# Transposing r and k of two chunks on TensorE in a fused RWKV-6 and feed-forward kernel, with a new instruction order

## The chip, the cores and the metric

The kernel runs on one core of a Trainium2 chip. Its time is the device time in microseconds of one execution. The kernel before took 179.31 us, the median of three runs (179.21 to 180.19).

## What is computed

For each batch and head, a linear attention with a decaying state runs over 768 positions; its output, all heads of a position side by side, goes through two matrix products with a leaky ReLU between them. The sizes are 4 batches, 8 heads, 768 positions and a head width of 48, so a row is 384 wide; the inner width is 2048.

```python
for t in range(S):
    cur = einsum('bhd,bhe->bhde', u * k[t], v[t])
    y[t] = einsum('bhd,bhde->bhe', r[t], state + cur)
    state = w[t][..., None] * state + einsum('bhd,bhe->bhde', k[t], v[t])
x = y.transpose(0, 2, 1, 3).reshape(3072, 384)
h = x @ w_in                      # 384 -> 2048
out = maximum(0.01 * h, h) @ w_out
```

All tensors are float32 in memory; the kernel computes its products in bfloat16.

## The kernel before

**Chunks.** The 3072 rows are cut into 24 chunks of 128 positions, numbered from zero in the order in which they are worked on (four batches take turns). Chunks 0 to 3 are worked on in pairs (`pair`), chunks 4 to 23 by `single`. The steps of a chunk are named here by the chunk and a short word: 6.k is the step of chunk 6 that makes its scaled k.

What a single chunk does, with the profile's lines and the engine:

- Four loads, w, k, r and v (L708, issued by SyncE), into one buffer `in`; lw, the logarithm of w (L718, ScalarE).
- cum: the running sums as a product (L724) and the chunk's totals (L727), TensorE; a: their exponentials (L745, ScalarE); ci: the sums less one position (L736, VectorE); two exponentials into PSUM (L750, L754, ScalarE).
- r and k: r and k times these exponentials (`mult`, L407, VectorE), into one tile `rk` of 128 positions by 2 x 512 in bfloat16 (each head is padded from 48 to 64).
- Then r and k are transposed into `rkT`, in one of two ways. On TensorE (`transposes`): four transposes of 128x128 for r and four for k (L418), each kind into one PSUM bank, and a copy out of PSUM for each kind, by VectorE (L423) or ScalarE (L425). Or by one DMA (L771) issued by SyncE, which transposes the whole of `rk` into `rkT`. The set `RK_DMA` names the chunks that go by DMA.
- scores: products of rkT's halves (L864), for one chunk or for two merged ones (10 with 11, 12 with 13 and others); two masks m (L795, VectorE); sb: the state scaled by a (L782, GpSimd); sums: k times v (L805, TensorE); state: sums plus sb (L820, VectorE; for a batch's first chunk a copy, L818); intra: the chunk's output (L831, L836, TensorE).
- The part of u: two products on GpSimd (L437, L441), their sum dg (L445, VectorE), vs: that times v (L449, GpSimd); vb: v in bfloat16 (L457, GpSimd).
- y: intra plus vs (L482, VectorE), its transposes (L468, TensorE) and the copy into xT (L473 VectorE or L475 ScalarE); six late chunks do this by DMA (L849).

**Blocks.** The feed-forward part goes by 14 blocks B0 to B13 of one or two chunks. A block has up products (L1030, into PSUM; the leaky ReLU by ScalarE, L1045) and down products (L1060, groups of four matmuls, then a copy into `o`, L1071 or L1073). Blocks B7 to B13 use, in place of the eight plain quarter products, seven products of sums and differences of quarters (L960, TensorE), with the sums made by VectorE (L941; in the weights once, L910, four steps) and the results taken by ScalarE and VectorE (L976, L974, L981). Weights come by DMA and are cast to bfloat16 (L340 to L344) by GpSimd, VectorE or ScalarE.

**Order.** All of it is cut into some 1,100 steps in `Plan`, each with the engine it may run on. The list `ORDER`, written out by number, gives the order in which the steps are emitted, so on each engine's queue the order of its steps; the table `FORCE` names the engine of a step that could run on several. A buffer is given to a step when it is emitted: eight PSUM banks `ps`, eleven buffers `in`, five `rk`, four `rkT`, and others. An engine takes its steps strictly in order and waits at one whose inputs or buffer are not ready. `Plan.order` also keeps times of its own for each step; they choose among free buffers and set the number of idle products that keep TensorE busy in the first 24 us.

Of the kernel before, what the change touches and what calls it, by code (L numbers as in the profile page):

```python
# [22 lines left out]
class Plan:  # L23
# [76 lines left out]
ORDER = [1122, 0, 1, 2, 3, 4, 5, 6, 7, 11, 14, 20, 12, 18, 15, 17, 16, 13, 19, 21, 8, 22, 25, 26, 27, 23, 36,  # L100
# [67 lines left out]
def kernel(  # L168
# [25 lines left out]
    RK_DMA = {6, 11, 12, 14, 15, 16, 17, 18, 19, 20, 21, 22, 23}  # L194
# [939 lines left out]
```

## Time and profile before

| | |
|---|---|
| median of three runs (lowest, highest) | 179.31 us (179.21, 180.19) |
| the profiled execution, first to last instruction | 177.0 us |
| mean granted TensorE clock | 1.000 |
| TensorE, its weight loads, VectorE, ScalarE, GpSimd busy | 96%, 79%, 81%, 64%, 61% |
| DMA transposes of rk | 13, a median of 3.8 us from issue to landing |
| moved by DMA | 34.25 MB, 115885 packets |

The profile names an execution's span from its first to its last instruction; the time of a run is longer by what lies around that. A group's row gives line, engine, operation, the tiles written and read, and their form; then the count, the busy time, the mean duration of one in nanoseconds, and the engine's idle time just before, with what ended it. A row of a timeline gives start, duration, and in brackets the idle time before. A matmul's end is modelled, since matmuls are pipelined: the drawn duration of one is longer than what it costs in a dense run. "PEld" is the loading of weights into TensorE, "SPq" the issuing of DMAs by SyncE.

### The profile page before, as it was taken

The numbers are of one execution on the slowest core, as the hardware profiler recorded it, in microseconds if no ns is written. First come the engines' busy times: TensorE is split into PE (matmuls) and PEld (weight loads), VectorE is DVE, ScalarE is ACT, GpSimd is POOL, SyncE is SP. The second block draws the span as 40 slices with busy tenths as digits, with TensorE's granted clock in tenths as the row PEclk, the third lists the DMA queues.
The fourth block names the chain that finished last, engine by engine and source line by source line (L and its number), as shares of the span: only waits on it lengthen the run. The fifth ranks groups of instructions, "written<-read, shape, count | busy, mean of one in ns | idle before, by whom it ended". The sixth has DMA issues, their size and how long they took to land.

```text
span 177.0 us, 5530 instructions
## 1 busy us (share of the span) xinstructions
PE 170.4 (96%) x2155; PEld 139.9 (79%) x2158; DVE 143.5 (81%) x299; ACT 114.0 (64%) x263; POOL 107.3 (61%) x143
## 2 busy tenths in 40 slices
PE   7999999999999999999999999999999998999993
PEld 2566779867768877777779899899899997799992
DVE  7498935267599899889879999999999999956662
ACT  5676769734677794796379964676769950178500
POOL 5989946486749859879599093391693959100000
PEclk9999999999999999999999999999999999999999
DMA  5999999999999999999999999996999897432104
GB/s 138 261 271 340 350 300 195 351 231 199 201 206 195 191 199 227 163 201 179 198 206 195 197 208 209 163 222 124 210 194 196 188 226 78 118 101 80 44 26 157
DMA packets 115885, 34.25 MB, mean 194 GB/s; under 512 B 108305, under 2 KB 115090, under 8 KB 115858
## 3 DMA queue, kind: packets, MB, share of 16 engines
q1 hardware_dynamic: 115856, 33.89, 93.1%
q8 instruction: 17, 0.28, 0.7%
q14 instruction: 10, 0.08, 0.2%
q10 hardware_dynamic: 2, 0.00, 0.0%
HBM read 25.17 MB, written 4.72 MB: 169 GB/s over the span
## 4 chain that ended last, share of the span: by engine, by line
PE 69%; DVE 15%; ACT 5%; issue 4%; DMA 3%; POOL 2%; DVEq 0%; SPq 0%; ACTq 0%
PE ps L1030 30%; PE ps L1060 13%; PE ps L960 10%; DVE rk L407 3%; DMA rkT<-rk 3%; PE ps L864 3%; DVE in L941 2%; PE ps L418 2%; ACT g L425 2%; PE ps L724 1%; PE ps L836 1%; DVE ci L736 1%; PE ps L518 1%; DVE dg L445 1%; ACT ps L750 1%
## 5 line engine op out<-in xcount | busy, mean ns | idle before, releaser
L1030 PE MATMUL ps<-xT,w_in_b 128*128 128x256 bf16 (+1 forms) x672 | 70.8, 258 | 0.3 <-DVE rk L407 0.2
L1045 ACT ACTIVATE g<-ps 128x512 bf16<-128x512 f32 x96 | 54.4, 598 | 18.1 <-PE ps L1030 16.0
L1030 PEld LDWEIGHTS <-w_in_b 128*128 128x128 bf16 x672 | 56.9, 98 | 7.8 <-issue 0.6
L437 POOL TENSOR_TENSOR ru<-in,ub 128x384 f32<-128x384 f32 x24 | 24.3, 1017 | 13.1 <-DMA in<-in_k_dram 7.0
L1060 PE MATMUL ps<-w_out_b,g 128*128 128x384 bf16 x160 | 31.4, 326 | 0.0
L407 DVE TENSOR_TENSOR rk<-in,ps 128x384 bf16<-128x384 f32 x48 | 24.8, 547 | 6.1 <-ACT ps L754 2.3
L782 POOL TENSOR_TENSOR sb<-s,a 128x384 bf16<-128x384 f32 x18 | 15.6, 875 | 16.6 <-ACT a L745 8.1
L795 DVE TENSOR_TENSOR m<-ps,maskb 128x512 bf16<-128x512 f32 x40 | 25.1, 682 | 0.3 <-PE ps L864 0.2
L441 POOL TENSOR_TENSOR ru<-ru,in 128x384 f32<-128x384 f32 x24 | 23.8, 1000 | 2.1 <-DMA in<-in_r_dram 1.1
L1060 PEld LDWEIGHTS <-g 128*128 128x128 bf16 x160 | 14.1, 97 | 6.8
L449 POOL TENSOR_TENSOR vs<-in,dg 128x384 f32<-128x384 f32 x20 | 17.4, 874 | 3.0 <-DMA in<-in_v_dram 2.1
L960 PEld LDWEIGHTS <-g 128*128 128x128 bf16 x224 | 18.3, 98 | 0.2
L976 ACT COPY o<-ps 128x192 f32<-128x192 f32 x18 | 5.8, 320 | 17.5 <-PE ps L960 15.5
L960 PEld LDWEIGHTS <-in 128*128 128x128 bf16 x168 | 13.6, 98 | 1.9 <-DVE in L941 1.4
L445 DVE TENSOR_REDUCE dg<-ru 128x8 f32<-128x384 f32 x24 | 12.9, 545 | 1.9 <-POOL ru L441 1.7
L457 POOL CAST vb<-in 128x384 bf16<-128x384 f32 x24 | 12.7, 534 | 2.2 <-DMA in<-in_v_dram 2.2
L981 DVE TENSOR_TENSOR o<-ps,o 128x192 f32<-128x192 f32 x35 | 11.6, 351 | 1.9 <-ACT o L976 1.1
L482 DVE TENSOR_TENSOR y<-ps,vs 128x384 bf16<-128x384 f32 x20 | 10.9, 553 | 2.4 <-PE ps L836 2.3
L754 ACT ACTIVATE ps<-ci 128x384 f32<-128x384 f32 x20 | 9.8, 493 | 4.7 <-DVE ci L736 4.1
L718 ACT ACTIVATE lw<-in 128x384 bf16<-128x384 f32 x20 | 9.9, 521 | 4.1 <-DMA in<-in_w_dram 4.1
L736 DVE TENSOR_TENSOR ci<-ps,lw 128x384 f32<-128x384 f32 x20 | 10.9, 551 | 1.8 <-PE ps L724 1.1
L960 PE MATMUL ps<-in,in 128*128 128x192 bf16 x112 | 11.4, 247 | 0.5 <-DVE in L941 0.5
(105 smaller groups left out, 258.8 us busy)
## 6 DMA issues: line engine op xcount, KB each, us to landing
out_dram<-o SPq DMA_DIRECT2D x23, 192.0 KB, 2.8
in<-in_w_dram SPq DMA_DIRECT2D x20, 192.0 KB, 4.7
in<-in_k_dram SPq DMA_DIRECT2D x20, 192.0 KB, 4.2
in<-in_r_dram SPq DMA_DIRECT2D x20, 192.0 KB, 4.2
in<-in_v_dram SPq DMA_DIRECT2D x20, 192.0 KB, 4.1
in<-in_moe_w_out_dram SPq DMA_DIRECT2D x4, 768.0 KB, 6.9
in<-in_moe_w_in_dram SPq DMA_DIRECT2D x2, 768.0 KB, 9.7
in<-in_moe_w_in_dram SPq DMA_DIRECT2D x4, 384.0 KB, 8.1
```

Source lines behind the costliest of these rows:

```text
L407: (nc.gpsimd if e == "POOL" else nc.vector).tensor_tensor(out=o, in0=x, in1=i, op=ALU.mult)
L437: lambda e: nc.gpsimd.tensor_tensor(out=ru.t[:], in0=kv(), in1=ubv, op=ALU.mult),
L441: lambda e: nc.gpsimd.tensor_tensor(out=ru.t[:], in0=ru.t[:], in1=rv(), op=ALU.mult),
L445: lambda e: nc.vector.tensor_reduce(out=dg.t[:], in_=ru.t[:], axis=AX.X, op=ALU.add),
L449: lambda e: nc.gpsimd.tensor_tensor(out=vs.t[:], in0=vv(), in1=dg.t[:].unsqueeze(2).to_broadcast([128, H, D]), op=ALU.mult),
L457: {"POOL": 0.56}, lambda e: nc.gpsimd.tensor_copy(out=vb.t[:], in_=vv()),
L782: lambda e: nc.gpsimd.tensor_tensor(out=sb.t[:].rearrange("p g a d -> p (g a) d"), in0=s_in.t[:].rearrange("p g a d -> p (g a) d"), in1=a_ ...
L795: lambda e, par=par: nc.vector.tensor_tensor(out=m.t[:, par, :, :], in0=sc[par].t[:].rearrange("p (g t) -> p g t", g=NP), in1=maskb[:].uns ...
L960: nc.tensor.matmul(o(), lhsT=x()[:, i, :], rhs=y()[:, i, :], start=fresh, stop=(stop and i == ii[-1]), skip_group_check=True)
L1030: nc.tensor.matmul(hp.t[:, a * N : (a + 1) * N], lhsT=w_in_b[:, t, (j + a) * 128 : (j + a + 1) * 128], rhs=xb.t[:, t, 0:N], start=(a == 0 ...
L1045: lambda e, hp=hp, g=g, j=j, J=J, N=N: nc.scalar.activation(out=g.t[:, j : j + J, 0:N], in_=hp.t[:, 0 : J * N].rearrange("p (a n) -> p a n ...
L1060: nc.tensor.matmul(op.t[:, 0:DM], lhsT=g.t[:, j, off : off + 128], rhs=w_out_b[:, j, :], start=(j == 0), stop=(j == NJ - 1))
```

## The change

Chunks 11 and 12 leave the set of those that are transposed by DMA:

```diff
-    RK_DMA = {6, 11, 12, 14, 15, 16, 17, 18, 19, 20, 21, 22, 23}
+    RK_DMA = {6, 14, 15, 16, 17, 18, 19, 20, 21, 22, 23}
```

For each of the two, one DMA step becomes four steps: transposes of r, a copy, transposes of k, a copy. The numbers of all later steps move up by three, then by six, and `ORDER` and `FORCE` are written anew:

```diff
-ORDER = [1122, 0, 1, 2, 3, 4, 5, 6, 7, 11, 14, 20, 12, 18, 15, 17, 16, 13, 19, 21, 8, 22, 25, 26, 27, 23, 36,
...
+ORDER = [1128, 0, 1, 2, 3, 4, 5, 6, 7, 11, 14, 20, 12, 18, 15, 17, 16, 13, 19, 21, 8, 22, 25, 26, 27, 23, 36, 40, 24,
...
-    "POOL", 122: "POOL", 124: "POOL", 126: "POOL", 128: "ACT", 129: "POOL", 131: "ACT", 132: "POOL", 134: "DVE",
-    135: "ACT", 137: "POOL", 138: "POOL", 140: "POOL", 141: "POOL", 143: "POOL", 144:
...
+    120: "POOL", 122: "POOL", 124: "POOL", 126: "POOL", 128: "ACT", 129: "POOL", 131: "ACT", 132: "POOL", 134: "DVE",
+    135: "ACT", 137: "POOL", 138: "POOL", 140: "ACT", 141: "ACT", 143: "POOL", 144: "DVE", 158: "ACT", 160: "DVE",
...
```

(Rows of `ORDER` and `FORCE` are shortened here.) Apart from the numbers, the first 201 entries of `ORDER` are the same; they reach to about 40 us. Behind them every engine's order differs, SyncE's excepted: its queue has the same steps in the same order, without the two DMA transposes. All four new copies out of PSUM are ScalarE's. Other steps also change engine: of the older copies of rkT five go from ScalarE to VectorE and three the other way; of those into xT three and two; of the copies into `o` (L1071, L1073) three from VectorE to ScalarE and one back; two states from VectorE to ScalarE; three copies of results (L976) from ScalarE to VectorE; two weight casts from GpSimd to ScalarE, and one from ScalarE to VectorE.

By name, the stretches of the queues that the prediction speaks of (dn1 is the second quarter of a block's down products, up4 its up products from the fifth on):

```text
TensorE from about 36 us
 before  4.scores B0.dn1 B2.dn1 B1.dn1 B0.dn2 5.tr 4.intra 4.sums B2.dn2 6.cum B1.dn2 B0.dn9 4.tr_y 5.tr B0.dn10
         B3.up4 B3.up12 B3.up0 B0.dn11 B1.dn3 7.cum 5.scores B0.dn3 B3.up8 B3.dn0 5.intra 7.tr B2.dn3 5.sums 7.tr
         B3.dn1 5.tr_y 8.cum 7.scores
 after   4.scores B0.dn1 B2.dn1 B0.dn9 B1.dn1 5.tr 4.intra 4.sums 5.tr B1.dn2 4.tr_y 5.scores B0.dn2 6.cum B0.dn10
         B3.up4 B3.up0 B2.dn2 B0.dn11 7.cum B1.dn3 B2.dn3 B3.up12 B3.dn0 B3.up8 B3.dn1 5.intra 5.sums B3.dn2 8.cum
         7.tr 7.tr 5.tr_y B3.dn3
VectorE from about 38 us
 before  5.r 5.copy 4.y 4.state 5.k 5.dg 6.ci 4.xT 5.copy 6.k 6.r 6.dg B0.o 7.ci 5.m 5.m 7.k 7.r 7.dg 5.y
 after   5.r 5.k 4.y 5.copy 4.xT 5.m 5.m 6.ci cast 5.dg 6.k 7.ci 6.r B1.o B2.o B0.o 7.k 7.r 5.y
GpSimd, chunks 10 to 14
 before  10.sb 11.ru 11.ruk 10.ru 10.ruk 13.ru 13.ruk 11.sb 10.vs 10.vb 12.ru 12.ruk 11.vs 11.vb 17.ru 12.sb 14.ru
         13.sb 14.ruk 12.vb 12.vs 13.vb 13.vs
 after   10.ru 10.ruk 11.sb 13.ru 10.sb 11.ru 10.vb 11.ruk 10.vs 12.sb 11.vb 11.vs 13.ruk 14.ru 12.ru 13.sb 12.ruk
         14.ruk 12.vb 12.vs 13.vb 13.vs
VectorE after, in the same stretch
         6.state 13.ci 11.m 10.m 11.m 13.k 10.m 13.r 12.ci 12.r 11.dg 10.y 12.k 10.xT 11.y L910 11.xT 13.dg 9.state
         11.state 12.m 12.m 13.m 14.ci 12.dg 15.ci 14.k 14.dg 14.r 13.m 13.state 13.y
```

(ru and ruk are L437 and L441.) In the order before, all four L910 steps stand behind 9.dg; in the new one they are spread over the stretch up to chunk 17. At the end, from 23.intra on, TensorE has the same products, with B12's and B13's up products in another order.

More of the change, by code (lines that the diff above doesn't have):

```diff
@@ L99 @@
 TY = (0.95, 24, 0.7, -0.6)
-ORDER = [1122, 0, 1, 2, 3, 4, 5, 6, 7, 11, 14, 20, 12, 18, 15, 17, 16, 13, 19, 21, 8, 22, 25, 26, 27, 23, 36,
[53 rows of a table removed]
-FORCE = {4: "ACT", 6: "DVE", 24: "ACT", 27: "ACT", 30: "DVE", 33: "ACT", 47: "ACT", 57: "ACT", 59: "DVE", 60:
-    "ACT", 62: "DVE", 80: "ACT", 83: "ACT", 86: "DVE", 89: "ACT", 103: "ACT", 113: "DVE", 115: "DVE", 116:
-    "DVE", 118: "DVE", 120: "POOL", 122: "POOL", 124: "POOL", 126: "POOL", 128: "ACT", 129: "POOL", 131: "ACT",
-    132: "POOL", 134: "DVE", 135: "ACT", 137: "POOL", 138: "POOL", 140: "POOL", 141: "POOL", 143: "POOL", 144:
-    "ACT", 158: "ACT", 160: "DVE", 169: "DVE", 173: "DVE", 187: "DVE", 189: "DVE", 198: "DVE", 202: "DVE", 238:
-    "ACT", 240: "ACT", 254: "DVE", 262: "ACT", 278: "ACT", 280: "ACT", 294: "ACT", 310: "DVE", 312: "ACT", 326:
-    "DVE", 342: "DVE", 344: "DVE", 378: "ACT", 386: "ACT", 422: "ACT", 424: "DVE", 438: "ACT", 446: "DVE", 495:
-    "ACT", 503: "ACT", 607: "ACT", 615: "ACT", 739: "ACT", 745: "DVE", 759: "ACT", 773: "DVE", 787: "DVE", 801:
-    "ACT", 823: "ACT", 829: "DVE", 851: "ACT", 857: "DVE", 885: "ACT", 888: "ACT", 893: "ACT", 921: "ACT", 924:
-    "ACT", 929: "ACT", 957: "ACT", 960: "ACT", 965: "ACT", 993: "ACT", 996: "ACT", 1001: "ACT", 1029: "ACT",
-    1032: "ACT", 1037: "DVE", 1065: "ACT", 1068: "ACT", 1073: "DVE", 1107: "DVE", 1110: "ACT", 1115: "ACT"}
@@ new lines @@
+ORDER = [1128, 0, 1, 2, 3, 4, 5, 6, 7, 11, 14, 20, 12, 18, 15, 17, 16, 13, 19, 21, 8, 22, 25, 26, 27, 23, 36, 40, 24,
[49 rows of a table added]
+FORCE = {4: "ACT", 6: "DVE", 24: "ACT", 27: "ACT", 30: "DVE", 33: "ACT", 47: "ACT", 57: "ACT", 59: "DVE", 60: "ACT",
+    62: "DVE", 80: "ACT", 83: "ACT", 86: "DVE", 89: "ACT", 103: "ACT", 113: "DVE", 115: "DVE", 116: "DVE", 118: "DVE",
+    120: "POOL", 122: "POOL", 124: "POOL", 126: "POOL", 128: "ACT", 129: "POOL", 131: "ACT", 132: "POOL", 134: "DVE",
+    135: "ACT", 137: "POOL", 138: "POOL", 140: "ACT", 141: "ACT", 143: "POOL", 144: "DVE", 158: "ACT", 160: "DVE",
+    169: "ACT", 173: "DVE", 187: "DVE", 189: "ACT", 198: "ACT", 202: "DVE", 238: "DVE", 240: "DVE", 254: "ACT", 262:
+    "ACT", 278: "DVE", 280: "DVE", 294: "ACT", 310: "ACT", 312: "DVE", 326: "ACT", 342: "DVE", 344: "DVE", 365: "ACT",
+    367: "ACT", 381: "DVE", 389: "DVE", 405: "ACT", 407: "ACT", 428: "ACT", 430: "ACT", 444: "ACT", 452: "DVE", 501:
+    "ACT", 509: "ACT", 613: "ACT", 621: "DVE", 745: "ACT", 751: "DVE", 765: "DVE", 779: "DVE", 793: "ACT", 807: "ACT",
+    829: "ACT", 835: "ACT", 857: "ACT", 863: "ACT", 891: "ACT", 894: "ACT", 899: "DVE", 927: "ACT", 930: "ACT", 935:
+    "DVE", 963: "ACT", 966: "ACT", 971: "ACT", 999: "ACT", 1002: "DVE", 1007: "ACT", 1035: "ACT", 1038: "ACT", 1043:
+    "DVE", 1071: "ACT", 1074: "ACT", 1079: "DVE", 1113: "DVE", 1116: "ACT", 1121: "ACT"}
```

102 rows, old and new, of the table ORDER are left out of this document.

## The prediction

> **What bounds the kernel now.** I read the page's busy times first, then the chain that ended last, then groups by form, then five places along the time axis.
>
> ```profile
> PE 170.4 (96%) x2155; PEld 139.9 (79%) x2158; DVE 143.5 (81%) x299; ACT 114.0 (64%) x263; POOL 107.3 (61%) x143
> DMA  5999999999999999999999999996999897432104
> PE 69%; DVE 15%; ACT 5%; issue 4%; DMA 3%; POOL 2%; DVEq 0%; SPq 0%; ACTq 0%
> 34.66 0.45 PE ps L418 x8
> 97.38 2.62 PE ps L1030 x24
> 166.09 7.93 PE ps L960 x96
> ```
>
> TensorE holds 69% of the chain. In the chain's dense pieces it issues without a hole: 2.62 us for 24 up products is 109 ns for 256 columns, 7.93 us for 96 products is 83 ns for 192, 0.45 us for 8 transposes is 56 ns for 128. All three are 0.43 ns a column, so the number of columns sets TensorE's time, and a transpose costs 56 ns wherever TensorE never waits. The DMA engines are nearly as full until about 145 us. The next view is by stretches (PE, PEld, DVE, ACT, POOL busy):
>
> ```profile
> 40.00:50.00 10.00, 9.69 (x115) 6.96 (x113) 7.14 (x16) 6.26 (x16) 7.48 (x9) 1.00 1.14 208
> 130.00:140.00 10.00, 10.00 (x129) 9.11 (x127) 9.82 (x21) 9.02 (x26) 6.95 (x8) 1.00 1.03 186
> 140.00:150.00 10.00, 9.82 (x141) 8.88 (x139) 9.97 (x18) 3.87 (x11) 8.12 (x12) 1.00 0.97 165
> ```
>
> From 130 to 150 us VectorE is as full as TensorE (19.8 of 20 us): there VectorE's backlog decides. Where TensorE does wait, the timeline shows it:
>
> ```profile
> 44.31 0.83 PE L1030 MATMUL ps<-xT,w_in_b 128*128 128x128 bf16 x12 [0.16 <-DVE rk L407]
> 46.94 0.82 PE L1060 MATMUL ps<-w_out_b,g 128*128 128x384 bf16 x4
> 47.69 0.83 PE L1030 MATMUL ps<-xT,w_in_b 128*128 128x128 bf16 x12
> 48.35 0.81 PE L1060 MATMUL ps<-w_out_b,g 128*128 128x384 bf16 x4
> 49.20 0.49 PE L836 MATMUL ps<-vb,m 128*128 128x48 bf16 x8
> 49.81 0.40 PE L418 MATMUL ps<-ident,rk 128*128 128x128 bf16 x4
> 150.38 0.84 PE L960 MATMUL ps<-in,in 128*128 128x192 bf16 x8 [0.53 <-DVE in L941]
> 151.61 0.83 PE L960 MATMUL ps<-w_out_b,in 128*128 128x192 bf16 x8 [0.40 <-DVE in L941]
> ```
>
> A matmul's end is modelled about 0.16 us behind the next one's earliest start (8 products of L960 are drawn as 0.84 us, but cost 8 x 83 ns = 0.66), so each hole is about 0.16 us longer than shown: 0.70 and 0.56 us at 150, 1.26 together. At 44 to 50 the holes are 0.32 at 44.31, then, from the starts (four down products cost 0.65 us, 12 half-width ups 0.66), 0.10 at 47.69, 0.20 at 49.20 and 0.4 at 49.81: 1.0 us. That is 2.3 us of waits behind the part that both orders share. Smaller ones are left out.
>
> **The transposes.** The two chunks' 16 transposes cost 16 x 56 ns = +0.9 us on TensorE, and nothing hides that: the number of the other matmuls is the same. Their four copies out of PSUM all go to ScalarE:
>
> ```profile
> L425 ACT COPY rkT<-ps 128x512 bf16<-128x512 bf16 x7 | 4.0, 590 | 0.9 <-PE ps L418 0.9
> L423 DVE COPY rkT<-ps 128x512 bf16<-128x512 bf16 x7 | 2.9, 420 | 4.4 <-PE ps L418 4.4
> L771 SPq DMA_TRANSPOSE rkT<-rk x13: 1232/1282/2201, 46.1 to 147.5; - x13
> 75.42 2.20 SPq L771 DMA_TRANSPOSE rkT<-rk  x1
> 77.72 1.15 SPq L708 DMA_DIRECT2D in<-in_k_dram  x2
> 81.76 2.11 SPq L771 DMA_TRANSPOSE rkT<-rk  x1
> ```
>
> Four times 590 ns is 2.4 us on an engine that is 64% busy; ScalarE's slack hides it, and without that slack it would cost 2.4. They also take four turns of the eight PSUM banks, for which no row here gives a price: from 0 to one hole of the size at 150 (0.70 us); I take 0, as no hole in the list stands at a transpose of r and k except at 49.81. SyncE loses two issues of 2.20 and 2.11 us (chunks 11 and 12) and the waits in front of them; the loads behind them keep their order and can start up to 4.3 us earlier. Nothing on TensorE waits for those loads directly, so I book no gain here, only that loads are not late (see the second rival). The Trainium skill, on the page VectorE: DVE Perf Modes, section The three transpose paths, gives 390 ns for a 128x128 transpose on TensorE and 1309 ns by DMA. By that, 16 would cost 6.2 us in place of 0.9, and the time would come out near 184; the row of eight in 0.45 us decides against it, since here they are issued back to back; I leave it a chance under 0.01.
>
> **The engines that change hands** in the new order: on VectorE two more copies of rkT (L423, 420 ns), one more of xT, one weight cast and three copies of L976 against two states and two o copies fewer: +0.6 us in all. ScalarE takes two weight casts from GpSimd (0.83 us each), ahead of a copy of 5's k and of 6.lw; there it sat idle:
>
> ```profile
> 39.42 0.52 ACT L718 ACTIVATE lw<-in 128x384 bf16<-128x384 f32 x1 [1.92 <-DMA in<-in_w_dram]
> ```
>
> The 1.92 us hold both casts; without that wait 5.scores would come up to 1.7 us later. SyncE's order is the same except for the two removed issues.
>
> **The order at 40 to 52 us.** VectorE's own idle time there:
>
> ```profile
> 43.70 0.56 DVE L407 TENSOR_TENSOR rk<-in,ps 128x384 bf16<-128x384 f32 x1 [1.04 <-ACT ps L754]
> 45.47 0.55 DVE L407 TENSOR_TENSOR rk<-in,ps 128x384 bf16<-128x384 f32 x1 [1.22 <-DMA in<-in_r_dram]
> 46.62 0.55 DVE L445 TENSOR_REDUCE dg<-ru 128x8 f32<-128x384 f32 x1 [0.59 <-POOL ru L441]
> 48.01 1.28 DVE L795 TENSOR_TENSOR m<-ps,maskb 128x512 bf16<-128x512 f32 x2
> 49.21 1.01 DVE L407 TENSOR_TENSOR rk<-in,ps 128x384 bf16<-128x384 f32 x2
> ```
>
> These are 6.k, 6.r and 6.dg, which wait for chunk 6's loads: 2.85 us idle. The new order moves 5.scores in front of 6.cum, so that both masks of chunk 5 (1.28 us, now at 48.01) and a weight cast (about 0.56) stand in front of 6.k and fill the wait, and 7.ci stands in front of 6.r. I take 1.5 of the 2.85 as saved (the bounds are 0 and 2.85; 7.ci waits for 7.cum, so not all). On TensorE, one more down product (0.65) stands in front of 5.intra, and 5.intra, 5.sums, a down product and 8.cum in front of 7's transposes, which covers the 0.20 and the 0.4; I take 0.7 of the 1.0 us as gone.
>
> **The order from 52 to 152 us.** I added up, from the mean durations, the work that each order puts ahead of a step on its own engine. TensorE's work ahead of the product at 150.38, less VectorE's work up to the difference that it reads: 15.7 us before, 15.6 after. For the one at 151.61: 15.3 and 16.2. TensorE's holes up to there equal VectorE's idle time less this lead, up to a constant. Before, the holes came to 1.0 + 0.7 = 1.7 at the first and 2.3 at the second. VectorE's idle time falls by 1.5 early and, I estimate, rises by 0.5 in the new, tight GpSimd stretch below: 1.0 less. So the first product's holes come to 1.7 + 0.1 - 1.0 = 0.8, the second's to 2.3 - 0.9 - 1.0 = 0.4, which the 0.8 covers. What remains is 0.8 or 0.9 of 2.3 us: -1.4. After 23.intra both orders run the same products, at full rate (the 96 above).
>
> **The sum.** +0.9 - 1.4 = -0.5 us. The profiled execution spans 177.0 us; the median of the three runs is 179.31, so 2.3 us lie around the span, which the change does not touch. 176.5 + 2.3 = 178.8 us. Half a per cent, 0.9 us, is about what a measurement of this kernel can tell from no change.
>
> **Rivals.** First, the whole 2.3 us goes, because VectorE's backlog is gone by 150: 177.0 + 0.9 - 2.3 + 2.3 = 177.9. For it speaks the full 2.85 us of early idle time; against it the lead at the first product, which does not grow. The Trainium skill points the same way: Perfetto Trace Analysis, section Identifying the Most-Contended Engine, says to judge TensorE by its weight loads and not by matmul time. By its 79% there would be room for 16 transposes at no cost, and with all holes gone the time would be 177.0; the dense rows at 0.43 ns a column leave no such room, and I give it 0.03, inside this rival's chance.
>
> Second, slower, by GpSimd. The new order moves 6.sums from 58 us to about 71 (12.7 us more TensorE work ahead), so 6.state ends near 74, and 10.sb, which waits for it, stands in GpSimd's queue ahead of 17 more steps of chunks 10 to 14.
>
> ```profile
> L437 POOL TENSOR_TENSOR ru<-in,ub 128x384 f32<-128x384 f32 x24 | 24.3, 1017 | 13.1 <-DMA in<-in_k_dram 7.0 <-issue 6.0
> L441 POOL TENSOR_TENSOR ru<-ru,in 128x384 f32<-128x384 f32 x24 | 23.8, 1000 | 2.1 <-DMA in<-in_r_dram 1.1
> L449 POOL TENSOR_TENSOR vs<-in,dg 128x384 f32<-128x384 f32 x20 | 17.4, 874 | 3.0 <-DMA in<-in_v_dram 2.1 <-DVE dg L445 0.9
> L457 POOL CAST vb<-in 128x384 bf16<-128x384 f32 x24 | 12.7, 534 | 2.2 <-DMA in<-in_v_dram 2.2
> L782 POOL TENSOR_TENSOR sb<-s,a 128x384 bf16<-128x384 f32 x18 | 15.6, 875 | 16.6 <-ACT a L745 8.1 <-ACT g L1045 4.6 <-DVE s L818 2.3
> 88.19 0.50 POOL L457 CAST vb<-in 128x384 bf16<-128x384 f32 x1 [0.91 <-DMA in<-in_v_dram]
> L736 DVE TENSOR_TENSOR ci<-ps,lw 128x384 f32<-128x384 f32 x20 | 10.9, 551 | 1.8 <-PE ps L724 1.1 <-PE ps L727 0.4 <-ACT a L745 0.2
> L482 DVE TENSOR_TENSOR y<-ps,vs 128x384 bf16<-128x384 f32 x20 | 10.9, 553 | 2.4 <-PE ps L836 2.3
> L910 DVE TENSOR_TENSOR in<-w_out_b 128x1536 bf16<-128x1536 bf16 x2 | 2.3, 1174 | 0.0
> ```
>
> Up to 13.vs that is 3 ru, 4 of L441, 3 sb, 4 vb and 4 vs: 3.05 + 4.00 + 2.63 + 2.14 + 3.50 = 15.3 us. VectorE's work from 6.state to 13.y, which needs 13.vs, is 4 ci, 8 masks, 6 rk, 4 dg, 2 y, 2 xT copies, one difference of L910 and 3 states: 17.8 us by the means, less some 0.08 for each of 30 that overlap (two masks in 1.28), 15.4. There is no slack, so 0.5 us of VectorE waits is in my sum. In this queue 12.vb comes 12.6 us behind 6.state, at 86.6; its load came at 88.1 before. If the two SyncE issues that are gone do not bring that load forward, VectorE loses 1.6 us there and TensorE gets it back as holes: 178.8 + 1.6 = 180.4. It decides from the point where v of chunk 12 lands behind about 86.6.
>
> Third, the order gains nothing: new holes take the place of the old ones, and the transposes are what is left: 179.31 + 0.9 = 180.2.
>
> **Chances.** The forecast 0.40 (its own range 178.2 to 179.6, of which 0.12 lies below 178.4), the first rival 0.20, the second 0.20, the third 0.20. Faster by over 0.5% is 0.20 + 0.12 = 0.32. Slower is most of the second, 0.17, and half of the third, 0.10: 0.27. The rest, 0.41, is no change. The range goes from the first rival with smaller holes closed too, 177.7, to the second with a further hole of 0.7 at a PSUM bank, 181.1.
>
> **What the profile after would show.** L418 with 104 matmuls and, in its dense pieces, still 56 ns each; 11 transposes on L771; the holes at 47 to 50 us gone, and 5.scores near 41; VectorE's idle time before 6.k under 1 us; holes in front of L960 near 150 of 0.5 us or so in all; v of chunk 12 landing before 87. The prediction is wrong if VectorE's idle time between 70 and 95 us grows by over 1 us, if a transpose into PSUM waits for a bank, or if the holes at 150 stay at 1.26.

## The result, and the profile after

The changed kernel takes 182.32 us (median of 13 runs, 181.16 to 184.67); the kernel before, on the same chip, 180.14 us (13 runs, 178.70 to 181.29). The ratio is 1.0128, with a 95% interval of 1.0091 to 1.0165: 2.2 us slower. Ratios here and below leave out a kernel's slow executions, those more than 1.5% above its fastest (here the one at 184.67). The prediction was 178.8 us, with a range of 177.7 to 181.1 about a kernel at 179.31; it was wrong in sign. The profiled execution of the changed kernel took 181.64 us and spans 179.9, 2.9 us more than the 177.0 of before.

In the changed kernel, and in all those of the experiments, every line number stands four lower (L418 is now L414, L1030 is L1026, L960 is L956). The page's busy times, then the groups that changed, then the line of the transposing DMA (count, then ns least/median/most, first and last start):

```profile
PE 171.3 (95%) x2171; PEld 140.3 (78%) x2174; DVE 144.4 (80%) x302; ACT 115.5 (64%) x266; POOL 108.7 (60%) x141
```

```profile
L414 PE MATMUL ps<-ident,rk 128*128 128x128 bf16 x104 | 9.1, 220 | 0.9 <-DVE rk L403 0.8
L421 ACT COPY rkT<-ps 128x512 bf16<-128x512 bf16 x9 | 5.2, 584 | 1.2 <-PE ps L414 1.2
L419 DVE COPY rkT<-ps 128x512 bf16<-128x512 bf16 x9 | 3.6, 416 | 4.1 <-PE ps L414 4.1
```

```profile
L767 SPq DMA_TRANSPOSE rkT<-rk x11: 1238/1686/2367, 46.9 to 149.8; - x11
```

The change did what it says: 104 transposes on TensorE instead of 88, 11 by DMA instead of 13. What matters is the 0.9 us in L414's last column, idle time in front of transposes that the prediction did not have. The next view, busy time by stretches, shows where idle time moved; first before, then after (columns as in the prediction: PE, PEld, DVE, ACT, POOL).

```profile
36.00:50.00 14.00, 13.69 (x157) 9.61 (x154) 10.14 (x21) 7.66 (x19) 10.90 (x14) 1.00 1.18 218
50.00:70.00 20.00, 20.00 (x267) 15.92 (x265) 19.03 (x35) 14.49 (x33) 14.78 (x18) 1.00 1.08 198
70.00:90.00 20.00, 20.00 (x232) 15.22 (x231) 17.58 (x36) 12.79 (x32) 15.97 (x21) 1.00 1.12 189
90.00:103.00 13.00, 13.00 (x166) 11.05 (x164) 11.10 (x22) 12.41 (x33) 8.07 (x11) 1.00 1.05 196
```

```profile
36.00:50.00 14.00, 13.76 (x154) 9.73 (x153) 10.36 (x21) 8.73 (x20) 7.40 (x9) 1.00 1.14 211
50.00:70.00 20.00, 19.54 (x271) 15.45 (x268) 16.48 (x34) 14.40 (x37) 14.28 (x19) 1.00 1.01 191
70.00:90.00 20.00, 19.37 (x241) 15.30 (x237) 17.14 (x33) 15.50 (x37) 16.96 (x19) 1.00 0.93 187
90.00:103.00 13.00, 13.00 (x148) 10.24 (x148) 11.85 (x22) 10.96 (x27) 10.89 (x13) 1.00 0.86 174
140.00:150.00 10.00, 9.21 (x131) 8.40 (x127) 9.89 (x17) 4.98 (x13) 8.43 (x10) 1.00 1.16 189
```

Read the third pair of figures, DVE. From 50 to 70 us VectorE was busy for 19.03 of 20 us and is now for 16.48: 2.55 us more idle, in a stretch in which the prediction quoted no waits. Over 36 to 103 us its idle time goes from 9.15 to 11.17 us. TensorE, drawn full from 50 to 90 before, now shows 1.1 us of holes there, and 0.8 from 140 to 150 instead of 0.2. The timeline names those holes (start, duration, in brackets the idle time before):

```profile
63.91 0.40 PE L414 MATMUL ps<-ident,rk 128*128 128x128 bf16 x4 [0.46 <-DVE rk L403]
72.52 0.38 PE L414 MATMUL ps<-ident,rk 128*128 128x128 bf16 x4 [0.38 <-DVE rk L403]
85.58 0.81 PE L1026 MATMUL ps<-xT,w_in_b 128*128 128x256 bf16 x6 [0.25 <-DVE xT L469]
143.19 0.40 PE L860 MATMUL ps<-rkT 48*128 48x128 bf16 x8 [0.49 <-DMA rkT<-rk]
150.51 0.83 PE L956 MATMUL ps<-w_out_b,in 128*128 128x192 bf16 x8 [0.80 <-DVE in L937]
```

From the starts of all matmuls I added up, for TensorE from 4.scores on, the time in which it had nothing to do, and what is left as its work:

| us | before | after |
|---|---|---|
| work | 135.06 | 135.97 |
| holes, 30 to 57 us | 1.15 | 0.63 |
| holes, 57 to 93 | 0.21 | 1.58 |
| holes, 93 to 130 | 0.22 | 0.40 |
| holes, 130 to 160 | 1.52 | 2.31 |
| holes, sum (with 0.04 behind 160 after) | 3.09 | 4.96 |

TensorE's part grows by 0.9 of work and 1.9 of holes; 4.scores starts 0.3 earlier, and behind TensorE's last matmul the span is 0.45 longer: 2.9 in all.

What lies behind the holes is seen on VectorE, then on GpSimd:

```profile
50.34 0.56 DVE L478 TENSOR_TENSOR y<-ps,vs 128x384 bf16<-128x384 f32 x1 [1.16 <-POOL vs L445]
51.67 0.36 DVE L469 COPY xT<-ps 128x384 bf16<-128x384 bf16 x1 [0.77 <-PE ps L464]
62.84 0.55 DVE L441 TENSOR_REDUCE dg<-ru 128x8 f32<-128x384 f32 x1 [1.04 <-POOL ru L437]
63.31 0.54 DVE L403 TENSOR_TENSOR rk<-in,ps 128x384 bf16<-128x384 f32 x1
69.66 0.54 DVE L403 TENSOR_TENSOR rk<-in,ps 128x384 bf16<-128x384 f32 x1
70.69 1.31 DVE L906 TENSOR_TENSOR in<-w_out_b 128x1536 bf16<-128x1536 bf16 x1
71.92 1.00 DVE L403 TENSOR_TENSOR rk<-in,ps 128x384 bf16<-128x384 f32 x2
```

```profile
60.85 1.00 POOL L433 TENSOR_TENSOR ru<-in,ub 128x384 f32<-128x384 f32 x1 [2.71 <-DMA in<-in_k_dram]
61.81 1.96 POOL L437 TENSOR_TENSOR ru<-ru,in 128x384 f32<-128x384 f32 x2
```

At 60.85 GpSimd stands at 9.ru, which waits 2.71 us for chunk 9's load of k. The new order has 8.ruk behind it, whose last input, r of chunk 8, had landed at 58.47; 8.ruk starts at 61.81. 8.dg on VectorE waits for 8.ruk (1.04 us), and behind 8.dg in VectorE's queue stands 9.r, whose transposes are TensorE's hole at 63.91. At 70.69 a difference of weights (L906, 1.31 us, due only much later) stands ahead of 10.k (71.92, the first of two in that row). The hole at 72.52 is in front of four of the sixteen new transposes, those of chunk 11's k. Their input, 11.k, had been ready since 70.20 (the row at 69.66). What they lacked was a PSUM bank: the kernel gives them the one in which the exponential for 10.k lies, and 10.k read it until 72.46. A second difference, at 84.07, stands ahead of 11's copy into xT and makes the hole at 85.58.

### The profile page after: what moved, and what is told of

Same layout as the page of the kernel before. It is cut to its first block, busy times and chain, and to the rows that moved or that the text cites. A ratio compares the mean times of both kernels' runs of the same rounds, so it can differ in the third digit from the quotient of the medians.

```text
span 179.9 us, 5549 instructions
## 1 busy us (share of the span) xinstructions
PE 171.3 (95%) x2171; PEld 140.3 (78%) x2174; DVE 144.4 (80%) x302; ACT 115.5 (64%) x266; POOL 108.7 (60%) x141
## 4 chain that ended last, share of the span: by engine, by line
PE 51%; SPq 13%; DMA 13%; POOL 8%; DVE 7%; issue 6%; ACT 0%; DVEq 0%; POOLq 0%
PE ps L1026 24%; PE ps L956 13%; DMA in<-in_k_dram 6%; SPq L490 5%; PE ps L1056 5%; SPq L314 4%; DMA in<-in_v_dram 4%; POOL ru L433 3%; DMA rkT<-rk 3%; SPq L704 2%; PE ps L860 2%; SPq L319 2%; POOL vs L445 2%; POOL ru L437 2%; PE ps L832 1%
## 5 line engine op out<-in xcount | busy, mean ns | idle before, releaser
L1026 PE MATMUL ps<-xT,w_in_b 128*128 128x256 bf16 (+1 forms) x672 | 72.4, 257 | 0.4 <-DVE xT L469 0.3
L1041 ACT ACTIVATE g<-ps 128x512 bf16<-128x512 f32 x96 | 55.1, 599 | 24.3 <-PE ps L1026 21.7
L1026 PEld LDWEIGHTS <-w_in_b 128*128 128x128 bf16 x672 | 56.0, 98 | 8.5 <-issue 1.2
L433 POOL TENSOR_TENSOR ru<-in,ub 128x384 f32<-128x384 f32 x24 | 25.0, 1047 | 15.0 <-DMA in<-in_k_dram 15.0
L403 DVE TENSOR_TENSOR rk<-in,ps 128x384 bf16<-128x384 f32 x48 | 25.3, 545 | 4.3 <-ACT ps L547 1.5
L437 POOL TENSOR_TENSOR ru<-ru,in 128x384 f32<-128x384 f32 x24 | 24.7, 1036 | 0.9
L778 POOL TENSOR_TENSOR sb<-s,a 128x384 bf16<-128x384 f32 x18 | 16.9, 949 | 7.9 <-DVE s L816 5.2
L445 POOL TENSOR_TENSOR vs<-in,dg 128x384 f32<-128x384 f32 x20 | 16.5, 828 | 7.9 <-DVE dg L441 4.5
L956 PEld LDWEIGHTS <-g 128*128 128x128 bf16 x224 | 18.4, 98 | 0.3
L956 PEld LDWEIGHTS <-in 128*128 128x128 bf16 x168 | 13.8, 98 | 1.4 <-DVE in L937 1.1
L441 DVE TENSOR_REDUCE dg<-ru 128x8 f32<-128x384 f32 x24 | 12.8, 543 | 1.4 <-POOL ru L437 1.4
L972 ACT COPY o<-ps 128x192 f32<-128x192 f32 x15 | 4.8, 319 | 14.2 <-PE ps L956 14.0
L741 ACT ACTIVATE a<-ps 64x4 f32<-64x4 f32 x36 | 6.0, 167 | 8.3 <-PE ps L723 3.8
L956 PE MATMUL ps<-in,in 128*128 128x192 bf16 x112 | 11.2, 246 | 0.0
```

The source lines that it names most:

```text
L403: (nc.gpsimd if e == "POOL" else nc.vector).tensor_tensor(out=o, in0=x, in1=i, op=ALU.mult)
L433: lambda e: nc.gpsimd.tensor_tensor(out=ru.t[:], in0=kv(), in1=ubv, op=ALU.mult),
L437: lambda e: nc.gpsimd.tensor_tensor(out=ru.t[:], in0=ru.t[:], in1=rv(), op=ALU.mult),
L441: lambda e: nc.vector.tensor_reduce(out=dg.t[:], in_=ru.t[:], axis=AX.X, op=ALU.add),
L445: lambda e: nc.gpsimd.tensor_tensor(out=vs.t[:], in0=vv(), in1=dg.t[:].unsqueeze(2).to_broadcast([128, H, D]), op=ALU.mult),
L778: lambda e: nc.gpsimd.tensor_tensor(out=sb.t[:].rearrange("p g a d -> p (g a) d"), in0=s_in.t[:].rearrange("p g a d -> p (g a) d"), in1=a_ ...
```

## The experiments

The theory behind the first five: the transposes cost 0.9 us as such, and the early misplacements just read cost the rest. All ratios are to the kernel before, run beside it on the same chip.

**E1: the order of before, only the transposes moved.**

```diff
- ORDER, FORCE: new
+ ORDER, FORCE: those of before; for the DMA step of 11 and of 12: transposes, copies (ScalarE)
```

> The order of before, with chunks 11 and 12 on TensorE: their DMA steps taken out, transposes of 11 put behind 13.cum, those of 12 behind the seventh up product of B6, the four copies on ScalarE right behind. Theory N (the new order makes the holes, the transposes cost their 16 x 56 ns): a ratio to before of 1.003 to 1.006, no hole at the transposes of 11 and 12. Theory T (the transposes, their PSUM banks and ScalarE's copies cost the time in any order): 1.010 or more, with holes at these transposes or at the scores behind them.

Measured: 180.51 against 178.87 us, 1.0091 (1.0041 to 1.0141). This lies between the two forecasts, and the interval holds both; the trace speaks for theory N, but the price of the transposes alone is no better known than 0.4 to 1.4%. TensorE's work in the profile is 135.85 us, so the +0.9 is the transposes' and not the order's. No hole stands at the transposes of 11 or 12. The holes, 4.19 in sum, hold one late load that the profile of before does not have:

```profile
41.01 0.32 PE L720 MATMUL ps<-lw,trev 128*128 128x384 bf16 x1 [1.57 <-ACT lw L714]
```

**E3, E4, E5: the new order with one or both misplacements mended.**

```diff
 VectorE (E3, E5)
- L906 first, 10.k, 10.r, ... L906 second, 11's copy into xT
+ 10.k, 10.r, L906 first, ... 11's copy into xT, L906 second
 GpSimd (E4, E5)
- 9.ru, 8.ruk
+ 8.ruk, 9.ru
```

> The changed kernel, with two L906 differences one or two places later on VectorE's queue: the first behind 10.r instead of in front of 10.k, the second behind 11's copy into xT instead of in front of it. Theory N: TensorE's holes at 72.5 (0.54 us) and 85.6 (0.42 us) go, and the ratio to before falls from 1.013 to about 1.008. Rival D (VectorE's and the loads' lateness decide the end, the holes only move): the two holes go, holes near 143 to 157 us grow by the same 0.9 us, ratio still 1.013.

> The changed kernel, with the second u product of chunk 8 (L437) in front of the first one of chunk 9 (L433) on GpSimd's queue, so that it no longer stands behind the load of 9's k. Theory N: VectorE's wait of 1.04 us before 8.dg and TensorE's hole of 0.62 us at 63.9 go, ratio 1.009 or 1.010. Rival D: the hole goes, the time stays.

> Both of the last two edits on the changed kernel. Theory N: three holes of 1.6 us in all go, ratio 1.004 to 1.006. Rival D: 1.011 to 1.013.

Measured: E3 1.0139 (1.0094 to 1.0184), E4 1.0099 (1.0049 to 1.0148), E5 1.0053 (1.0011 to 1.0095), all on one chip. The transposes of 11's k, with a hole of 0.38 at 72.52 in the changed kernel, in E4 and then, with both edits, in E5 (second row):

```profile
71.84 0.38 PE L414 MATMUL ps<-ident,rk 128*128 128x128 bf16 x4 [0.84 <-DVE rk L403]
```

```profile
70.27 0.81 PE L1056 MATMUL ps<-w_out_b,g 128*128 128x384 bf16 x4
70.92 0.39 PE L414 MATMUL ps<-ident,rk 128*128 128x128 bf16 x4
```

E4 closed the hole at 63.91, and the one at 72 grew: what TensorE did not lose first it lost at the next tight place. With both edits TensorE's holes from 57 to 93 us are 0.29 instead of 1.58, and the loss falls from 1.3% to 0.5%, as E5's theory N had it. The drawn idle time from 130 to 157 us did not take the gain back (1.08 us against 1.44 in the changed kernel). The two edits are shown together; singly they are not resolved. E3's time is its rival's (1.013), though the holes it aimed at are gone; its profile has 1.7 us of late loads at 40 us, which cover them. Kernels that share this early part and differ only late, E7, E13 and E10 below, stand at 1.0067 (1.0038 to 1.0096), 1.0083 (1.0053 to 1.0114) and 1.0111 (1.0064 to 1.0158).

**E2: the mended order with chunks 11 and 12 by DMA again** (the DMA steps right ahead of the scores that read them).

> The kernel with both edits, but chunks 11 and 12 transposed by DMA again, in the new order: the DMA steps stand right in front of the scores that read them. If the transposes on TensorE cost 16 x 56 ns and nothing else, TensorE's work from 4.scores on is 135.1 us as before, 0.9 less than with them. The DMA takes 3 to 5 us, and the new order has these scores 3 to 5 us behind r and k: holes of 0 to 3 us at the two merged scores, ratio 1.00 to 1.02. Above 1.005 the new order rests on the transposes on TensorE; below, it does not need them.

Measured: 1.0174 (1.0139 to 1.0208). TensorE's work is 135.00 us, without the 0.9, but its holes are 7.5, 2.76 of them from 57 to 93:

```profile
82.87 0.34 PE L464 MATMUL ps<-ident,y 128*128 128x128 bf16 x3 [0.32 <-DVE y L478]
84.15 0.36 PE L832 MATMUL ps<-vb,m 128*128 128x48 bf16 x8 [0.77 <-POOL vb L453]
```

So nothing shows the new order to be better in itself: by DMA it loses 1.7%, with the DMAs at this one place in the queue, and what it may gain over the old one with the transposes on TensorE, 1.0053 against 1.0091, lies within the intervals.

**E6 to E11: closing the remaining holes one at a time** (from E5; E6: 4.vb ahead of 4.vs on GpSimd; E7: B9's store behind 21's transposing DMA; E8: four copies of rkT to ScalarE; E9: the first 50 us much as before; E10: E7 with B10's last sum five steps earlier; E11: E9's and E10's edits).

> The kernel with both edits (L906 later, 8's second u product earlier), and the cast of chunk 4's v (L453) in front of its product vs (L445) on GpSimd's queue, as in the order before. Theory N: TensorE's hole of some 0.4 us at 38 to 39, in front of 4.intra, goes, and with it 0.4 us of the time. Rival D (the backlog of VectorE decides the end): that hole goes, those from 130 to 160 us grow by as much.

> The kernel with both edits, and the store of a half of B9 one place later on SyncE's queue, behind the DMA transposes of chunk 21, which it held up. Theory S (the hole of 0.7 us inside the merged scores near 142 us is SyncE's queue): the transposes of 21 land about 1 us earlier, the hole goes, 0.7 us less. Rival D: the hole goes, the one near 148 us in front of L956 grows by as much.

> The kernel with both edits, and the four copies of rkT of chunks 8 and 10 on ScalarE instead of VectorE: 4 x 420 ns less on VectorE between 55 and 80 us, 4 x 590 ns more on ScalarE. Theory D (TensorE's holes near 150 us are VectorE's backlog, carried along from earlier): the hole of 0.47 us at 148 goes and those behind it shrink. Theory N or S: these holes stay as they are, since other things make them.

> The kernel with both edits, and the stretch at 38 to 43 us put back nearer to the order before: 5.k behind 4's copy into xT on VectorE, the transposes of 5's k behind three down products and 6.cum on TensorE, 4.vb in front of 4.vs, 4.state earlier. Theory L (the new order put 5.k and 5.scores right behind the load of 5's k, which lands up to 2 us later in some runs): VectorE's wait for that load (0.9 to 2.5 us in the new order's profiles) and TensorE's holes of 0.4 to 2 us at 38 to 41 go, the runs lie closer together, ratio 1.001 to 1.003. Rival D: the holes go, later ones grow by as much, ratio 1.005 to 1.007.

> The kernel with both edits and the later store of B9, in which the only large hole is 1.4 us at 149 us, in front of the last L960 product of B10; here VectorE makes the sum that this product reads (L937) five steps earlier, in front of B11's first. Theory P (one step's place on VectorE's queue makes that hole): the hole goes, nothing takes its place, ratio 0.998 to 1.001. Rival D (VectorE is the bound from 103 to 150 us, whatever the order within): holes of the same sum in front of the next steps that read VectorE's work, B11's products near 151 or chunk 20's and 21's outputs, ratio 1.005 to 1.007.

> All edits together, those of the early stretch and that of B10's sum. Theories L and P: holes of 1 us or less in all, TensorE's work 0.9 us above that of before, ratio 0.993 to 0.998, so faster than both kernels. Rival D: 1.002 to 1.005.

Measured: E6 1.0100 (1.0036 to 1.0164), E7 1.0067, E8 1.0153 (1.0111 to 1.0194), E9 1.0132 (1.0092 to 1.0172), E10 1.0111 (1.0064 to 1.0158), E11 1.0152 (1.0111 to 1.0193). In E7, E9 and E10 the hole aimed at went; none gained. In E8 and E11 late holes stay (0.53 at 143.94 and 0.32 at 150.78 in E8; 0.57, 0.74 and 0.57 from 149.78 on in E11). E9's first 50 us have new holes for ScalarE (0.48 and 0.69 us at 41.57 and 45.40), and E8 gave ScalarE copies for which it had no time: at 75.45 TensorE waits 0.71 for it. E5 at 148 us, then E7, then E10:

```profile
148.31 0.83 PE L956 MATMUL ps<-w_out_b,in 128*128 128x192 bf16 x8 [0.31 <-DVE in L937]
```

```profile
148.81 0.83 PE L956 MATMUL ps<-w_out_b,in 128*128 128x192 bf16 x8 [1.20 <-DVE in L937]
```

```profile
149.63 0.33 PE L827 MATMUL ps<-sb,rkT 128*128 128x96 bf16 x4 [0.47 <-DVE rk L403]
151.56 0.82 PE L956 MATMUL ps<-in,in 128*128 128x192 bf16 x8 [0.74 <-DVE o L970]
152.71 0.50 PE L956 MATMUL ps<-in,in 128*128 128x192 bf16 x4 [0.32 <-DVE in L937]
```

E7 took away the wait for 21's DMA (0.62 at 141.49 in E5), and TensorE reached B10's products earlier and waited longer for their sum. E10 moved the sum up, and three other VectorE steps were late in its place; its execution also waits 0.85 us at 137.85 and 0.83 at 40.53, behind late loads. E7 and E10 read as one lag, TensorE's over VectorE, that appears wherever the next meeting of the two is. For the other late holes this is not shown.

**E12 to E15: is it the work that the new order gave VectorE late?** The new theory: from the first mask of chunk 15 to the last of 23 VectorE has hardly a pause, and the new order gave it more to do there, among it four steps from ScalarE (three takes of L972 and 19's copy into xT). The line of the masks shows the first and last start; before, then after:

```profile
L795 DVE TENSOR_TENSOR m<-ps,maskb x20: 676/680/692, 103.1 to 153.5; 128x512 bf16<-128x512 f32 x20
```

```profile
L791 DVE TENSOR_TENSOR m<-ps,maskb x20: 674/678/690, 103.3 to 156.7; 128x512 bf16<-128x512 f32 x20
```

50.4 us before, 53.4 after: 3.0 us more, and the span grew by 2.9.

```diff
 FORCE: takes of B7, B8, B10 and 19's copy into xT
- DVE   (E12: the changed kernel; E13, E14: E5)
+ ACT   (E14 also moves one L906 ahead of the first mask of 15)
 E15: the kernel before, the same four
- ACT
+ DVE
```

> The changed kernel with four steps back on the engine that has them before: the three takes of L976 (products of B7, B8 and B10) and chunk 19's copy into xT go from VectorE to ScalarE, in the same places of the order. Theory (VectorE is the bound from 103 us on, and its amount of work there sets the end): VectorE's stretch from the first mask of chunk 15 to the last mask of chunk 23 falls by about 1.4 us from 54.05, and the time from 1.013 of the kernel before to about 1.005. Rival (the order within that stretch makes the holes, and the amount does not count): the stretch loses its work but gains idle time, and the ratio stays at 1.012 or more.

> The kernel with both early waits mended (the two differences of L906 moved back, 8.ruk ahead of 9.ru), which stood at 1.005, and the same four steps back on ScalarE. Theory (VectorE's amount of work behind 103 us): mask 15 to mask 23 in 52 to 53 us, TensorE's idle time from 130 us on from 2.1 to about 1 us, ratio 0.997 to 1.000. Rival (order within the stretch): ratio stays at 1.005.

> The kernel of the run before, and one more difference of L906 (0.6 us of VectorE) done ahead of the first mask of chunk 15, where VectorE still has idle time. Theory (amount of work behind 103 us): another 0.6 us off the stretch, ratio lower by 0.003 than that kernel's. Rival (order): no difference, or a new wait ahead of 103 us and a higher ratio.

> The kernel before, its order and its DMA transposes untouched; only the engine of those four steps is changed, from ScalarE to VectorE. Theory (amount of VectorE's work behind 103 us): the stretch from mask 15 to mask 23 grows by about 1.4 us from 51.1, ratio 1.006 to 1.009. Rival (the new order makes the loss and not where four steps run): ratio 0.998 to 1.003, with VectorE's work taken up by its idle time.

Measured: E12 1.0141 (1.0106 to 1.0177), E13 1.0083 (1.0053 to 1.0114), E14 1.0122 (1.0082 to 1.0163), E15 1.0126 (1.0084 to 1.0167). The masks run from 102.8 to 155.9 in E12 (53.1), 103.0 to 155.3 in E13 (52.3), 103.6 to 155.4 in E15 (51.8). The two sides disagree: giving VectorE the four steps costs the kernel before 1.3%, taking them away gives the changed one nothing in time. E15's span is 2.0 us longer than that of before. Of these 0.5 lie ahead of the first mask, where TensorE waits 1.32 us at 41.53 for a late load; its stretch grew by 1.4, as its theory had it, and the trace shows where:

```profile
147.69 0.82 PE L956 MATMUL ps<-in,in 128*128 128x192 bf16 x8 [2.28 <-DVE o L970]
```

```profile
144.89 2.48 DVE L791 TENSOR_TENSOR m<-ps,maskb 128x512 bf16<-128x512 f32 x4
147.28 0.35 DVE L970 COPY o<-ps 128x192 f32<-128x192 f32 x1
```

The same copy before, by ScalarE:

```profile
143.53 0.32 ACT L976 COPY o<-ps 128x192 f32<-128x192 f32 x1
```

A copy of 0.35 us stands behind four masks, and the next product waits 2.28 us for it. Before, ScalarE had it done by 143.85, and no product waited. In the changed kernel's trace no product waits for such a copy, so E12 had nothing to win. In E13's trace the late idle time did fall as its theory had it; E5, then E13, TensorE's busy time being the second figure:

```profile
103.00:157.00 54.00, 52.92 (x706) 48.01 (x704) 52.20 (x106) 30.22 (x76) 32.47 (x38) 1.00 0.89 167
```

```profile
103.00:157.00 54.00, 53.56 (x714) 48.84 (x713) 51.90 (x102) 31.34 (x81) 34.07 (x40) 1.00 0.97 174
```

That is 0.64 us less idle, but E13's execution lost 1.65 us at 39 to 41 us to late loads (last section), and its times show no gain. By the times, the four steps are not what the changed kernel lost by; whether they cost the mended order something stays open.

**E16 to E18: the early part of one order joined to the late part of the other**, cut at the first mask of 15 (E16: mended new, then old; E17: old, then new; E18: old up to 6's load of k, mended new up to the mask, old behind). Transposes on TensorE in all three; a step that would find no free buffer at the seam comes a few places later.

> Transposes of chunks 11 and 12 on TensorE in both this kernel and the next two. Here the steps up to the first mask of chunk 15 stand in the new order (with both early waits mended), and all behind it in the old order with the old engines; four steps at the seam (VectorE's 17.ci, a difference of L906, 12's state, 16's k) change sides. Theory (the late part of the order, with the steps that it leaves to VectorE there, costs 2 to 3 us, whatever the early part): mask 15 to mask 23 in 51 to 51.6 us on VectorE instead of 53.8, its start 0.5 to 1.2 us later, ratio 0.995 to 1.001. Rival (the late holes are carried over from the early part: loads, buffers, banks): the stretch stays over 53 us, ratio 1.005 or more.

> The mirror: the old order up to the first mask of chunk 15, the new order (and its engines) behind it. Theory: mask 15 to mask 23 in 53.5 to 54.5 us although the early part is the old one, ratio 1.012 to 1.020 (the old order with the transposes alone stood at 1.009). Rival (carried over from the early part): about 51.1 us and 1.009.

> As the first of these, but the steps up to the load of k of chunk 6 (some 40 us) in the old order too, so that 5's product with k does not stand right behind its load: only the middle, 40 to 103 us, is new. Theory: the stretch as in the first, 51 to 51.6 us; whether the start is earlier or later than there tells what the new order's first 40 us are worth; ratio 0.994 to 1.003. Rival (the early part of the new order is what made the start early): start later by over 0.7 us and ratio above the first's by 0.004.

Measured: E16 1.0160 (1.0126 to 1.0194), E17 1.0304 (1.0256 to 1.0352), E18 1.0262 (1.0233 to 1.0292). Masks of E16, then E17, then E18:

```profile
L791 DVE TENSOR_TENSOR m<-ps,maskb x20: 675/681/691, 106.6 to 156.9; 128x512 bf16<-128x512 f32 x20
```

```profile
L791 DVE TENSOR_TENSOR m<-ps,maskb x20: 673/680/685, 104.1 to 159.3; 128x512 bf16<-128x512 f32 x20
```

```profile
L791 DVE TENSOR_TENSOR m<-ps,maskb x20: 675/681/692, 107.7 to 158.4; 128x512 bf16<-128x512 f32 x20
```

The stretch is 50.3 us in E16 and 50.7 in E18, with the old late part, as in the kernel before and in E1 (both 50.4). It is 55.2 in E17, with the new one (E17's seam makes TensorE wait 1.90 us at 104.22), and 52.3 to 54.7 in every other kernel with the new one. So its length goes with the late part of the order, whatever stands ahead: that half of the theory held. But its price did not. E16 ends its masks at 156.9, no earlier than the changed kernel at 156.7, because its first mask starts 3.3 us later: three VectorE steps and several TensorE steps of blocks B7 and B8 that the new order leaves behind the mask stand ahead of it here, and the seam adds 2.6 us of TensorE waits between 104 and 109. My forecast of 0.995 to 1.001 failed, and so did those of E17 (1.012 to 1.020) and E18 (0.994 to 1.003). The length of a stretch between two marks says nothing alone when steps can cross the marks.

## Why the prediction was wrong

**The transposes: right.** +0.9 us predicted as 16 x 56 ns. TensorE's work grew by 135.97 - 135.06 = 0.91; it is 135.7 to 136.0 in every kernel with them and 135.0 to 135.1 in the three without (before, E2, E15). The figure of 390 ns in the Trainium skill (VectorE: DVE Perf Modes, The three transpose paths) would have shown as 6.2 us; 0.91 / 16 = 57 ns did. The other page of the Trainium skill that was weighed, Perfetto Trace Analysis (Identifying the Most-Contended Engine), judges TensorE by its weight loads and by MFU, the operations done against the peak, which is not worked out here. The weight loads at 79% were read as room; the work came in full, at 78%.

**The early holes: about right.** 0.7 us of 1.0 was to go; from 30 to 57 us 1.15 became 0.63. VectorE does not wait at 6.k, and 5.scores runs at 40.56, as forecast.

**The step that failed: "VectorE's idle time falls by 1.5 early and, I estimate, rises by 0.5", from there carried through to 150 us.** The time saved before 47 us was handed back by 52: VectorE then stood ahead of GpSimd and waited 1.16 us for 5.vs and 0.77 for TensorE. Then came 8.dg's 1.04 us behind 9.ru, which the prediction did not look for: it counted the GpSimd queue from 6.state to 13.vs and not the one at 60 us, where the order of two steps and one load decide. Added up to the difference that the product near 150 reads, VectorE's idle time since 36 us rose from 10.5 to 12.2 us, by 1.7, where a fall of 1.0 had been put in. TensorE's holes up to that product grew by about as much. But the product that decided was another than the two of B11 for which the leads had been worked out: B10's last (150.51), whose last sum ran at 141.31 before, ahead of the four masks of 20 and 21, and runs at 149.69 now, behind them.

**A term put at nothing: the PSUM banks.** For the four turns of the banks the prediction took 0, with 0.70 us as the most. One turn did cost: the transposes of 11's k waited for a bank at 72.52, 0.38 us as drawn and 0.54 in the prediction's measure. "If a transpose into PSUM waits for a bank" was one of its own signs of being wrong. E5 has the same bank and no hole there, so the price came from the difference put ahead of 10.k, not from the turn alone. Of the two other signs, VectorE's idle time from 70 to 95 us fell (3.83 to 3.47 us), and near 150 one hole of 0.96 (0.80 as drawn) stands where 1.26 was and 0.5 was forecast.

**"What remains is 0.8 or 0.9 of 2.3 us: -1.4"** is the term of the sum that this turned over: the holes rose by 1.9. The engine swaps, booked at 0.6 us of VectorE work, were not the cause in this order (E12); E15 shows that they could have been, at 2.1 us (181.23 against 179.15). The 2.3 us that "lie around the span" were wrong as well: in every execution on record the time is 1.7 to 1.9 us above the span. The profiled execution of before, some 178.7 by that, was as fast as the fastest of its 13 runs (178.70), which is why the spans differ by 2.9 us and the medians by 2.2.

**The rivals.** The third, "the order gains nothing", 180.2 or 1.005, is about where the mended order ends (1.0053, 1.0067 and 1.0083 in E5, E7 and E13; the six others with both mends and more steps moved, E6, E8 to E11 and E14, stand at 1.0100 to 1.0153). The rest of the loss, some 0.5 to 0.7% by those three, goes with the two misplacements. The second rival did not occur as put: v of chunk 12 landed at 87.25, behind its turning point of 86.6, but GpSimd reached 12.vb only at 89.72, so nothing waited for the load, and VectorE's idle time from 70 to 103 us did not grow (4.32 to 4.01 us). But its kind, a GpSimd queue in which one step waits for a load and holds up another chunk's, did occur, at 60 us.

**What stays open.** Whether the mended order costs anything beyond the 0.5% of the transposes, which the intervals of E5, E7 and E13 do not settle, and which late waits a third order could remove: of six attempts (E6 to E11) none gained. No kernel beat the one before.

## What to carry to other kernels

When two engines are both over 90% full, count the idle time of both over the whole path, in every stretch: a wait removed early is worth only what no third engine takes back a few microseconds later. In a strictly ordered queue, check for each step the load that it waits for and what of another chunk stands behind it; two such misplacements cost more here (1.3 us of holes) than sixteen transposes (0.9). A step that frees a PSUM bank is priced by the queue in front of it, not by its own time: a copy of 0.35 us cost TensorE 2.28 us behind four masks, and transposes whose input was ready waited for a bank that 10.k had still to read. So for each new use of a bank, look up whose bank it is.

## What was not expected of the hardware

The same instructions can meet their loads 1.8 us later in one execution than in another. E5 and E13 are the same up to 103 us; in E5 5.k starts at 38.35, in E13 at 40.19 behind its load; TensorE then stands for 0.62 and 1.03 us, and the first mask of 15 starts at 103.0 instead of 101.5. VectorE in E5, VectorE in E13, TensorE in E13:

```profile
38.35 0.56 DVE L403 TENSOR_TENSOR rk<-in,ps 128x384 bf16<-128x384 f32 x1 [0.83 <-ACT w_out_b L340]
```

```profile
40.19 0.56 DVE L403 TENSOR_TENSOR rk<-in,ps 128x384 bf16<-128x384 f32 x1 [2.50 <-DMA in<-in_k_dram]
```

```profile
39.24 0.36 PE L832 MATMUL ps<-vb,m 128*128 128x48 bf16 x8 [0.62 <-POOL vb L453]
40.80 0.40 PE L414 MATMUL ps<-ident,rk 128*128 128x128 bf16 x4 [1.03 <-DVE rk L403]
```

The first mask's 1.5 us are 0.8% of the span, more than most differences here, so two single profiles are compared stretch by stretch behind the last such wait, and times only by medians. The order of before meets late loads too: in E1, E15, E17 and E18, whose first 40 us are its own, TensorE waits 1.57, 1.32, 1.49 and 1.72 us at about 41 us, behind a load of w. In the profiles of before and after, on which the account rests, it waits at most 0.19 us between 38 and 42 us.

The median issue of a transposing DMA rose from 1282 to 1686 ns in the changed kernel. The smaller number of them is not the reason: E1 has the same eleven.

```profile
L767 SPq DMA_TRANSPOSE rkT<-rk x11: 1232/1280/2280, 45.9 to 148.6; - x11
```

What lengthens some of them is not shown.
